# Transposed value weights of a backward kernel: DMA transposes from DRAM in place of TensorE transposes

## The chip, the cores and the metric

The kernel runs on one NeuronCore of a Trainium2 chip. The metric is device time in microseconds (us) of one execution; three executions before the change took 2987.54, 2988.93 and 2990.67 us, so the median is 2988.93 us. A core has a matrix engine (PE, TensorE), whose weight loads are shown apart (PEld), a vector engine (DVE), a scalar engine (ACT), a general one (POOL) and a sync engine (SP) that issues DMAs. SP, ACT and POOL each have their own DMA queue; sixteen DMA engines move the data of all queues.

## The reference, cut to what matters

The kernel computes the forward pass and all weight and input gradients of a transformer block. Half A is a recurrent-memory attention (32 heads of 128, model width 512, 2048 rows in segments of 32 with 8 memory rows); half B is a gated linear unit (GLU) of width 1792.

```python
def _A_ref(x, mem0, Wq, Wk, Wv, Wo, seg_len):      # Wq, Wk, Wv: [512, 32, 128]
    for s in range(n_seg):
        h = jnp.concatenate([mem, xs], axis=1)
        q = jnp.einsum('btd,dhe->bhte', h, Wq)
        k = jnp.einsum('btd,dhe->bhte', h, Wk)
        v = jnp.einsum('btd,dhe->bhte', h, Wv)
        ...
        o = jnp.einsum('bhte,hed->btd', o, Wo)
        mem = o[:, :M, :].copy()
def _B_ref(x, w_gate, w_up, w_down):
    h = _sigmoid(jnp.einsum('bsd,df->bsf', x, w_gate)) * jnp.einsum('bsd,df->bsf', x, w_up)
    return jnp.einsum('bsf,fd->bsd', h, w_down)
...
_out, _vjp = jax.vjp(_f, A_x, A_mem0, A_Wq, A_Wk, A_Wv, A_Wo, B_w_gate, B_w_up, B_w_down, c, w_mod)
_grads = _vjp(grad_out)
```

The gradient of `h` in half A needs products with the transposed weights, such as `dv` times `Wv` with `d` as the result's axis. For these the kernel keeps `WqT`, `WkT` and `WvT` in SBUF, each 128 partitions (the head's axis `e`) by 32 heads by 512, and `WoT` likewise. They are made from the weights in DRAM; what is at issue here is how `WvT` is made.

## The kernel before, in words

The work comes in stages one after the other: forward attention (phase 2), the GLU forward and its input gradients (phase 3), the GLU weight gradients with the making of the transposed weights (the stage of this case, lines 1426 to 1489), the attention backward over the 64 segments in reverse (phase 4), and the attention's weight gradients (phase 5).

**The stage.** The gradient of `w_down` is finished first (line 1369). Then, from 1342.6 to 1471.6 us of the profiled span, come the gradients of `w_gate` (from `DGROWS`) and `w_up` (from `DUROWS`). Each is cut into four column chunks of 448. The text calls them DG0 to DG3 and DU0 to DU3. A chunk is four groups `c` of 16 matmuls (line 1470): `h2r` as weights, a chunk `xr` of the rows as the moving operand, into a PSUM tile `gps` of which there are four. Each group's result is copied out by ACT or DVE in turn (`ot`, two tiles) and stored by a DMA on POOL's queue. A chunk of rows is 1792 KB in DRAM; there are two such tiles in SBUF (`ring`), and `load_xr` (line 1448) issues the load of chunk i+2 on ACT's queue when the matmuls of chunk i have all read. After DU0 and DU1, 16 matmuls of the first attention backward step are put in (`first_dO_pass`), and after DU2 eight transposes (`first_dO_turns`).

**The weight pieces.** Between the groups, PE makes the transposed weights in 32 pieces of four heads, handed out evenly over the stage by `emit_setup`: eight of `Wq`, eight of `Wo`, eight of `Wk`, eight of `Wv`. A piece of `Wq`, `Wk` or `Wv` is one DMA on SP's queue of 512 KB from DRAM into one of four slots (line 1559), 16 transposes on PE (line 1564, four to a PSUM tile `wtp`, of which there are two), and four copies of 128 by 512 from PSUM to `WqT`, `WkT` or `WvT`, two of three on DVE and the third on ACT. A slot's next load waits until the transposes of the piece four places before have read it, so SP runs about four pieces ahead of PE.

**What sets the order.** SP's order in this stage is pinned to the order of the code. A scheduler orders the other engines and gives each DMA of SP and ACT one of eight completion semaphores (in the built program `DMAHW0` to `DMAHW7`), shared by the two queues. A DMA waits before it is issued until the DMA that had its semaphore before has landed. An engine works strictly in its own order, so whatever stands behind a waiting DMA on ACT or SP waits too.

**After the stage.** Phase 4 first loads `Pst`, `OT`, `Qst` and `Kst` on SP's queue and `VT` on ACT's; `WvT` is first read by PE at 1478.98 us of the profiled span (line 215).

The text calls the pieces of `Wk` K0 to K7 and those of `Wv` V0 to V7.

Of the kernel before, what the change touches and what calls it, by code (L numbers as in the profile page):

```python
# [40 lines left out]
class K:  # L41
# [1496 lines left out]
    def p4_weights_setup_pieces(self, ctx):  # L1538
        nc, tc, cfg, io = self.nc, self.tc, self.cfg, self.io
        D, DC, H, E = cfg.D, cfg.DC, cfg.H, cfg.E  # L1540
        HB = 4
        sps = ctx.enter_context(tc.tile_pool(name="p4sps", bufs=2, space=PSUM, reuse_waits="tile"))
        pieces = []
        kk = [0]
        n, NT = DC * HB * E, cfg.NT
        slots = [self.flat(self.Wv, 2 * NT * 448, n)] + [self.flat(self.Wk, i * n, n) for i in range(3)]
        first = [slots[0], self.flat(self.Wk, NT * D, n), slots[0], slots[0]]
        np_ = [0]

        def slot(pat, **kw):  # L1550
            np_[0] += 1
            t = first[np_[0] - 1] if np_[0] <= 4 else slots[(np_[0] - 4) % 4]
            return t.rearrange(pat, **kw)

        def qkv_piece(src_ap, dst, h0):
            def f():
                srcv = src_ap.rearrange("(c p) h e -> p c h e", p=128)
                wn = slot("p (c h e) -> p c h e", c=DC, e=E)
                nc.sync.dma_start(wn, srcv[:, :, h0:h0 + HB, :])
                for hi in range(HB):  # L1560
                    h = h0 + hi
                    tp = sps.tile([128, DC, 128], BF16, name="wtp")
                    for c in range(DC):
                        nc.tensor.transpose(tp[:, c, :], wn[:, c, hi, :], self.ident[:])
                    self.evac("dve" if kk[0] % 3 != 2 else "act", dst[:, h, :], tp[:, :, :].rearrange("p c d -> p (c d)"))
                    kk[0] += 1
            return f

        def wo_piece(h0):
            def f():  # L1570
                wov = io["A_Wo"].rearrange("h e d -> e h d")
                won = slot("p (h d) -> p h d", h=HB)
                nc.sync.dma_start(won, wov[:, h0:h0 + HB, :])
                for c in range(DC):
                    tp = sps.tile([128, HB, 128], BF16, name="wtp")
                    for i in range(HB):
                        nc.tensor.transpose(tp[:, i, :], won[:, i, c * 128:(c + 1) * 128], self.ident[:])
                    self.evac("dve" if kk[0] % 3 != 2 else "act", self.WoT[:, c, h0 * E:(h0 + HB) * E],
                              tp[:, :, :].rearrange("p i e -> p (i e)"))
                    kk[0] += 1  # L1580
            return f

        for (src_ap, dst) in ((io["A_Wq"], self.WqT), (None, None), (io["A_Wk"], self.WkT), (io["A_Wv"], self.WvT)):
            for h0 in range(0, H, HB):
                pieces.append(wo_piece(h0) if dst is None else qkv_piece(src_ap, dst, h0))
        return pieces

    def p4_weights_setup_transposes(self):
# [817 lines left out]
```

## Time and profile before

| what | value |
|---|---|
| median of three runs | 2988.93 us |
| the profiled execution | 2995.39 us, span 2993.6 us |
| PE busy over the span | 2930.3 us (98%) |
| transposes of line 1564 | 384 (128 of them for `Wv`), 1303.4 to 1469.0 us |
| matmuls of line 1470 | 512, 1342.6 to 1471.3 us |
| loads of the DUROWS chunks, issued on ACT's queue | 1389.69, 1404.74, 1420.99, 1438.84 us |
| loads of `Wv` pieces, issued on SP's queue | 1418.5 to 1452.6 us |
| mean granted TensorE clock | 0.995 of full speed |

The profile has one row of records for each engine. Times are from the start of the span. A matmul's listed duration overlaps with the next one's, so the cost of a group is read from one start to the next, not from the durations' sum. "Granted clock" is the share of full speed at which TensorE was clocked in that stretch. The DMA share is the mean busy share of the sixteen DMA engines, and can exceed 1 where packets overlap.

### The profile page before, as it was taken

How to read it: one execution, taken by the hardware profiler on the slowest of the kernel's cores; microseconds unless marked ns; L12 is line 12 of the kernel's file. 1: busy time of each engine (PE TensorE's matmuls, PEld its weight loads, DVE VectorE, ACT ScalarE, POOL GpSimd, SP SyncE). 2: the span in 40 equal slices, each digit the busy share in tenths (PEclk: the TensorE clock that was granted, in tenths of full speed). 3: DMA queues.
4: the chain of work that ended last, by engine and by line, in shares of the span. 5: the costliest groups of instructions: out<-in, count | busy, mean ns of one | idle time of the engine just before them, and what ended most of it. 6: DMA issues, size and time to landing. Idle time of an engine off the chain costs nothing. (4 is left out here: it accounts for less than half of the span.)

```text
span 2993.6 us, 105831 instructions
## 1 busy us (share of the span) xinstructions
PE 2930.3 (98%) x43947; PEld 1838.7 (61%) x44021; DVE 1631.3 (54%) x3679; ACT 1271.0 (42%) x3057; POOL 1233.4 (41%) x2489
## 2 busy tenths in 40 slices
PE   6999999999999999999999999999999999999999
PEld 3666666666665544445677777677777754445544
DVE  5656666665655788833456565566556632750011
ACT  2555555555555533312355555455555520110011
POOL 2455555545555222221244444444444422762111
PEclk8999999999999999999999999999999999999999
DMA  9988988889989899998699999999999997786565
GB/s 306 213 226 216 211 214 224 210 218 214 210 215 271 214 233 229 230 282 281 201 247 251 250 252 250 243 252 251 252 253 253 248 280 247 250 263 190 162 213 168
DMA packets 836436, 703.04 MB, mean 235 GB/s; under 512 B 536642, under 2 KB 708850, under 8 KB 835060
## 3 DMA queue, kind: packets, MB, share of 16 engines
q1 hardware_dynamic: 710756, 486.09, 66.3%
q0 software_dynamic: 54640, 148.90, 15.9%
q10 hardware_dynamic: 70560, 61.28, 6.4%
q8 instruction: 346, 5.67, 0.8%
q14 instruction: 134, 1.10, 0.1%
HBM read 294.99 MB, written 276.35 MB: 191 GB/s over the span
## 5 line engine op out<-in xcount | busy, mean ns | idle before, releaser
L2187 PE MATMUL gps<-rows,hrows 128*128 128x512 bf16 (+2 forms) x2124 | 413.6, 355 | 1.9
L2187 PEld LDWEIGHTS <-hrows 128*128 128x128 bf16 x2160 | 211.2, 98 | 204.4 <-issue 0.9
L63 DVE CAST ot<-gps 128x512 bf16<-128x512 f32 (+3 forms) x76 | 48.2, 634 | 304.3 <-PE gps L2187 221.0
L1855 POOL COPY dOst<-RAd 96x512 bf16<-96x512 bf16 x128 | 75.2, 611 | 299.4 <-DVE RAd L63 297.3
L1038 POOL TENSOR_TENSOR Pst<-Pst,rden 120x1408 bf16<-120x1408 bf16 x63 | 159.7, 2535 | 83.9 <-issue 53.6
L61 ACT ACTIVATE ot<-gps 128x512 bf16<-128x512 f32 (+3 forms) x75 | 41.2, 549 | 349.9 <-PE gps L2187 220.1
L2191 POOL DMA_DIRECT2D out_dram<-ot x108 | 81.4, 754 | 260.2 <-DVE ot L63 137.0
L659 PE MATMUL pass_ps<-Wv,hT 128*32 128x512 bf16 (+2 forms) x2304 | 186.6, 357 | 0.0
L257 PEld LDWEIGHTS <-hT 128*32 128x32 bf16 x4096 | 115.2, 97 | 103.2 <-issue 6.0
L63 DVE CAST Vst<-pass_ps 96x512 bf16<-96x512 f32 x128 | 87.4, 683 | 106.7 <-ACT RBv L61 92.9
L215 PE MATMUL dh_ps<-WvT,dVT 128*32 128x512 bf16 x2048 | 133.9, 381 | 1.7
L223 PE MATMUL at_ps<-Wo,OT 128*32 128x256 bf16 x4096 | 124.6, 274 | 4.0 <-DMA Wo<-in_A_Wo_dram 3.4
L257 PE MATMUL pass_ps<-Wq,hT 128*32 128x512 bf16 x2048 | 124.0, 383 | 4.1 <-DMA Wq<-in_A_Wq_dram 4.1
L659 PE MATMUL pass_ps<-Wv,hb 128*32 128x512 bf16 (+2 forms) x636 | 127.2, 345 | 0.0
L257 PE MATMUL pass_ps<-Wk,hT 128*32 128x512 bf16 x2048 | 123.5, 383 | 2.5 <-POOL hT L549 1.1
L257 PE MATMUL pass_ps<-WoT,dyT 128*32 128x256 bf16 (+1 forms) x3072 | 122.7, 308 | 2.8 <-issue 2.0
L223 PE MATMUL dhq_ps<-WqT,dQT 128*32 128x256 bf16 x4096 | 122.9, 273 | 0.0
L215 PE MATMUL dh_ps<-WkT,dKT 128*32 128x512 bf16 x2048 | 122.3, 380 | 0.0
L2202 PE MATMUL gps5o<-WoT,rows 128*128 128x512 bf16 x549 | 120.4, 379 | 1.7 <-DMA rows<-OSR 1.1
L794 POOL DMA_DIRECT2D Vst<-RBv x192 | 99.6, 523 | 53.9 <-ACT ET L841 34.5
L223 PEld LDWEIGHTS <-dQT 128*32 128x32 bf16 x4096 | 110.0, 97 | 15.5
L315 DVE TENSOR_TENSOR dST<-dh_ps,dST 128x512 bf16<-128x512 f32 x64 | 44.3, 691 | 130.3 <-ACT dST L314 130.3
(472 smaller groups left out, 7037.8 us busy)
## 6 DMA issues: line engine op xcount, KB each, us to landing
OSR<-Ost SPq DMA_DIRECT2D x64, 352.0 KB
OT<-OT SPq DMA_DIRECT2D x64, 352.0 KB
PS<-Pst SPq DMA_DIRECT2D x64, 352.0 KB
Pst_l<-PS SPq DMA_DIRECT2D x64, 352.0 KB
OT_l<-OT SPq DMA_DIRECT2D x64, 352.0 KB
DVR<-rows_x POOLq DMA_DIRECT2D x64, 352.0 KB, 6.5
DKR<-rows_x POOLq DMA_DIRECT2D x64, 352.0 KB, 5.9
DQR<-rows_x POOLq DMA_DIRECT2D x64, 352.0 KB, 3.3
```

Of the source, the lines that this page charges most:

```text
L63: return nc.vector.tensor_copy(out, in_)
L215: self.nc.tensor.matmul(ps[32 * j:32 * j + 32, :], lhsT=lhsT, rhs=w, start=(n < 4), stop=(n >= total - 4), tile_position=(0, 32 * j))
L223: nc.tensor.matmul(ps[32 * j:32 * j + 32, :], lhsT=x[k], rhs=w[k][:, 256 * d:256 * d + 256], start=(n == 0), stop=(n == total - 1), tile_p ...
L257: self.nc.tensor.matmul(ps[32 * j:32 * j + 32, :], lhsT=lhs(c), rhs=rhs, start=(c == 0), stop=(c == DC - 1), tile_position=(0, 32 * j))
L315: nc.vector.tensor_tensor(lo, ps[:], hi, op=ALU.subtract)
L659: nc.tensor.matmul(ps[32 * j:32 * j + 32, o * E:(o + n) * E], lhsT=lhsT, rhs=wc[:, 3 * a + hl:3 * (a + n - 1) + hl + 1:3, :], start=(c == ...
L794: nc.gpsimd.dma_start(Vst[96 + 8 * j:104 + 8 * j, :], rb[32 * j + o:32 * j + o + 8, :])
L1038: nc.gpsimd.tensor_tensor(Pst[0:120, :, :], Pst[0:120, :, :], rden[:, :].unsqueeze(2).to_broadcast([120, G, 128]), op=ALU.mult)
L1855: nc.gpsimd.tensor_copy(dOst[0:96, 512 * hf:512 * hf + 512], RAd[0:96, 512 * hf:512 * hf + 512])
L2187: nc.tensor.matmul(ps[:, 0:ng * E], lhsT=hrows[:, tp_, c * 128:(c + 1) * 128], rhs=rows[:, tp_, 0:ng * E], start=(tp_ == 0), stop=(tp_ == ...
L2191: nc.gpsimd.dma_start(outw[c * 128:(c + 1) * 128, h0:h0 + 3 * (ng - 1) + 1:3, :], ot[:, 0:ng * E].rearrange("p (h e) -> p h e", e=E))
L2202: nc.tensor.matmul(pss[gg][:], lhsT=rows[:, t, gg * E:(gg + 1) * E], rhs=dyrows[:, t, :], start=(n == 0), stop=(n == NTP - 1))
```

## The change

The pieces of `Wv` are no longer loaded plainly and transposed by PE. Each is instead four DMA transposes on SP's queue, straight from DRAM into `WvT`: 128 rows by 512 columns (128 KB) that land as four blocks of 128 by 128. That is 32 DMA transposes for 8 plain loads, 128 PE transposes and 32 copies out of PSUM. The order of the pieces changes too: `Wq`, `Wo`, K0 to K3, and then four times one piece of `Wk` followed by two of `Wv`. The number of pieces and how `emit_setup` hands them out stay as they are, but the last twelve places now hold only four pieces with work for PE.

```diff
+        def dma_piece(src_ap, dst, h0):
+            def f():
+                for c in range(DC):
+                    nc.sync.dma_start(dst[:, h0:h0 + HB, c * 128:(c + 1) * 128],
+                                      src_ap[c * 128:(c + 1) * 128, h0:h0 + HB, :].rearrange("p h e -> p (h e)"), transpose=True)
+            return f
+
+        heads = range(0, H, HB)
+        pieces = [qkv_piece(io["A_Wq"], self.WqT, h0) for h0 in heads] + [wo_piece(h0) for h0 in heads]
+        ks = [qkv_piece(io["A_Wk"], self.WkT, h0) for h0 in heads]
+        vs = [dma_piece(io["A_Wv"], self.WvT, h0) for h0 in heads]
+        pieces += ks[:4]
+        for i in range(4):
+            pieces += [ks[4 + i], vs[2 * i], vs[2 * i + 1]]
-        for (src_ap, dst) in ((io["A_Wq"], self.WqT), (None, None), (io["A_Wk"], self.WkT), (io["A_Wv"], self.WvT)):
-            for h0 in range(0, H, HB):
-                pieces.append(wo_piece(h0) if dst is None else qkv_piece(src_ap, dst, h0))
         return pieces
```

In the built program the rest of the instructions keep their order on every engine. The semaphores of the stage's DMAs are handed out anew. The load of DU1's rows now has the semaphore that V0's first transpose had before it (`DMAHW4`), the load of DU2's rows that of V5's third transpose (`DMAHW5`), and the load of DU3's rows that of V6's second (`DMAHW1`). Before the change, the loads of DU1 to DU3 shared theirs with the loads of O6, K2 and K6 (O6 the seventh piece of `Wo`), all issued more than 8 us earlier.

## The prediction

> **What bounds the kernel now.** I read the page's busy rows first, then the line of the transposes, the order in time on PE, SP and ACT between 1380 and 1480 us, and last the stretches' DMA share and clock.
>
> ```profile
> PE 2930.3 (98%) x43947; PEld 1838.7 (61%) x44021; DVE 1631.3 (54%) x3679; ACT 1271.0 (42%) x3057; POOL 1233.4 (41%) x2489
> L1564 PE MATMUL wtp<-ident,Wv x128: 216/219/219, 1303.7 to 1469.0; 128*128 128x128 bf16 x128
> ```
>
> PE is busy nearly always, so a transpose taken out of its stream counts, if nothing else ends the stage later. The order in time on PE (start, duration, what) gives the price:
>
> ```profile
> 1432.19 2.62 PE L1470 MATMUL gps<-Wv,Wk 128*128 128x448 bf16 x13
> 1434.64 0.61 PE L1564 MATMUL wtp<-ident,Wk 128*128 128x128 bf16 x8
> ...
> 1436.18 2.62 PE L1470 MATMUL gps<-Wv,Wk 128*128 128x448 bf16 x13
> 1438.73 1.05 PE L257 MATMUL pass_ps<-WoT,dyb 128*32 128x512 bf16 x16
> 1439.71 3.20 PE L1470 MATMUL gps<-Wv,Wk 128*128 128x448 bf16 x16
> ```
>
> Thirteen matmuls take 2.45 us from start to start (1432.19 to 1434.64), so one takes 0.189 us and a group of 16 takes 3.03. V0's stretch, 1434.64 to 1438.73, holds 16 matmuls and 16 transposes: 4.09 us, so the piece costs 1.06.
>
> The moving rows come on ACT's queue, and nothing waits for them now: of 512 matmuls one waited 0.4 us. DU2's load is the third line:
>
> ```profile
>   DMA Wv<-DGROWS: 0.4, 1
> 1404.74 0.37 ACTq L1448 DMA_DIRECT2D Wv<-DUROWS  x1
> 1420.99 0.37 ACTq L1448 DMA_DIRECT2D Wv<-DUROWS  x1
> 1399.43 13.31 SPq L1559 DMA_DIRECT2D Wk<-in_A_Wk_dram  x3
> L1197 SPq DMA_TRANSPOSE hdT<-h x14: 1201/1202/1227, 994.6 to 1242.5; - x14
> 1424.00:1426.00 2.00, 2.00 (x12) 1.07 (x11) 0.00 (x0) 0.31 (x1) 0.00 (x0) 1.00 1.10 386
> ```
>
> ACT's queue moves data for DU2's load from 1422.2 to 1429.7 us (the DMA queues by single microseconds), so it lands about 8.7 us after its issue and 10.0 us before DU2's first matmul at 1439.71. SP issues K4's load at 1399.43. The nearest row to the new DMAs is `hdT<-h`: the same 128 by 512 into four blocks, but out of SBUF; it holds SP for 1.20 us. A full-rate plain load moves 386 GB/s (last number).
>
> **The change part by part.** The profiled execution took 2995.39 us (span 2993.6), 6.5 us or 0.22% above the median of 2988.93. All terms are differences, so I add them to the median. About 0.2% (6 us) is what a measurement of this kernel can tell from no change.
>
> *Taken off PE.* Eight pieces. From one piece's first transpose to the next's, less 3.03 us for 16 matmuls (and 0.45 for the eight turns after DU2), V0 to V7 cost 1.06, 1.07, 0.95, 0.96, 1.01, 1.21, 0.89, 1.08: together 8.2. Small waits between stretches of matmuls add a few tenths; I take **-8.6**, as laying out the stage anew gives it (below). The 32 copies out of PSUM (0.42 us on DVE, 0.60 on ACT) and eight plain loads (0.37 us each on SP) go too. Those engines were waiting for PE here, so they save nothing.
>
> *Added on SP.* 32 DMA transposes of 128 KB. Plain loads of DRAM and stores to DRAM hold their issuer equally long (0.37 and 0.36 us), so I carry the 1.20 us over from an SBUF source to a DRAM source; two in a row start 1.29 us apart (1242.55, 1243.84). 32 make 41 us of SP. They do not run in the last quarter: SP is not held back until a place comes up, but only by the slots of K4 to K7, and those are free when K0 to K3 are turned, which K4's issue at 1399.43 shows for K0. So V0 is issued at 1399.9 and the rest follow at SP's pace. Data: in a stretch with little else, transposes move 190 to 233 GB/s, so 4.19 MB need 20 us of all DMA engines where plain loads needed 11. Spread over 41 us this is half of them. While DU1's load also runs (7 us at full share), 128 KB at half of 190 GB/s take 1.38 us, 0.09 more than an issue, which delays the stream by some **0.5**.
>
> *The wait that it adds.* This decides. In the built program DU2's load, on ACT's queue, has taken over the completion semaphore of V5's third transpose and waits until that has landed. That is the 23rd transpose. With K5's and K6's loads between (0.46 each), its issue ends at 1399.9 + 23 x 1.29 + 0.9 + 0.5 = 1431.0. Data of an `hdT` transpose run 0.7 us from the end of issue; `rows_x<-dQT` among other loads was landed 4.4 us after it (issue to 2431.79, its reader at 2436.22). I take 2.5, so 1433.5, where ACT could issue at 1420.99 before. Behind the wait on ACT stand the copies of DU1's first and third group, of the first pass and of one head of K5, and DU3's load. POOL's stores wait for these copies and DVE's copy of the fourth group for a store. But there are four `gps` tiles and two `wtp`, so PE gets through DU1 and stops only where it needs DU2's rows. These take 8.7 us as now, or with nine transposes beside them some 9: landed at 1442.5.
>
> *PE anew.* DU0 ends at 1420.8 as now (V0 would stand behind it). The first pass takes 1.0, DU1 64 x 0.189 + 1.0 for K5 = 13.1, the second pass 1.0: PE wants DU2's rows at 1435.9 where it wanted them at 1439.7. From there DU2, turns and DU3 with K6 and K7 take 26.8, so without a wait the stage ends at 1462.7 to 1463 instead of 1471.57 (the -8.6). With rows at 1442.5 PE stands still for **+6.6**.
>
> *The clock after it.* When PE stood 1.6 us after several smaller gaps, its clock was 0.50 from 1477 to 1480:
>
> ```profile
> 1476.07 0.37 PE L1810 MATMUL g_ps<-Pst_l,dOst 128*128 128x120 bf16 x4 [1.57 <-DMA Pst_l<-PS]
> 1477.00:1477.50 0.50, 0.50 (x8) 0.50 (x6) 0.19 (x1) 0.04 (x1) 0.00 (x0) 0.50 0.83 274
> 1480.50:1481.00 0.50, 0.50 (x13) 0.07 (x6) 0.00 (x0) 0.00 (x0) 0.00 (x0) 1.00 0.97 355
> ```
>
> 3.6 us at half clock are **+1.8** after a stand of 6.6 us. That dip itself, at phase 4's start, stays: its cause is the load of `Pst`, which waits for PE's last `gps` matmul as before.
>
> *The rest.* DU1's load waits for V0's first transpose, landed by 1403.6, before its own time of 1404.74: nothing. DU3's load waits for V6's second, landed near 1438, and then follows DU2's on the queue, landed near 1449 for a need at 1456: nothing, with 7 us of cover. K5 to K7 are issued at 1410, 1421 and 1432, each over 10 us before its turn. `WvT` is complete near 1446, read at 1479.
>
> Sum: -8.6 + 6.6 + 1.8 = **-0.2 us**, so 2988.7.
>
> *The unknown price.* The trace has no DMA transpose out of DRAM. Each 0.1 us on the interval moves the end by 2.3. From below, the issue of a copy (0.37) would leave the data rate (128 KB at 190 GB/s, 0.69) as the bound: V5's third would land at 1419, no wait. From above, the slowest transpose that shows is `duT<-du` at 1277.85, 448 KB in 6.08 us, or 1.74 for 128 KB, 1.83 with the gap: +12.4; landing at 4.4 instead of 2.5 adds 1.9. I take 1.29 as the row of the same shape, and keep both ends.
>
> The Trainium skill (DMA: Bandwidth & Descriptors, the table within "Why a DMA increments its semaphore by 16 and not by 1") gives the issue of a small DMA transpose from HBM to SBUF as 631 cycles before trn3; at the 1.2 GHz that its page Trainium Kernel Development and Optimization (NeuronCore Architecture) gives for SyncEngine, I estimate 0.53 us from the two pages. No run here shows it. By it the sum would be -8.6.
>
> **The rivals.**
>
> *Transposes out of DRAM are issued quickly.* Mechanism: the 23rd transpose lands before DU2's load needs to go. With the interval at or below 1.0 us it lands at 1427, and rows are there at 1436: the gain is whole, 2988.9 - 8.6 = **2980.3**. It decides below 1.08, where wait and dip leave less than -6. For it: a copy is issued in 0.37, so the 1.20 is work on transposing, which may be cheaper from DRAM. Against: `hdT<-h` never took under 1.20.
>
> *Transposes out of DRAM are slower, so the wait of DU2's load outgrows the gain.* Place: ACT's queue ahead of DU2; price 2.3 us for each 0.1; it decides from 1.56 us on (+6). At 1.83 and a late landing: 2988.7 + 12.4 + 1.9 = **3003**. For it: 256-byte packets (3146 of 3170 packets under 512 bytes while transposes ran) read out of rows 8 KB apart; the medians of 1.80 and 2.02 us for `rows_x` of 352 KB among other traffic. Against: those are 2.75 times as much data.
>
> *The wait binds nothing.* If DU2's load went at 1421 as now, the result would be that of the first rival; only the semaphore's count speaks against it, and I fold it in there.
>
> **How the numbers follow.** Wait about as long as the gain: 0.42, **2988.7**, its own range 2983 to 2995. Quick issue: 0.22. Slow: 0.36. The range leaves 0.1 below for nothing but scatter of the first rival, hence 2979, and 0.1 above, beyond the slow rival's 3003, hence 3008. Faster by over 0.2%: 0.23; within: 0.41; slower: 0.36.
>
> **What would show it.** No line for `Wv` among the transposes, PE's stage after 1399 shorter by 8.6 us of work; SP's transposes 1.2 to 1.3 us each from 1399.9 on; DU2's load issued near 1433 and not 1421, at the landing of the 23rd; one wait of PE of some 7 us at line 1470 for the rows of `DUROWS`; a granted clock of 0.5 for 3 to 4 us behind it. I am wrong if DU2's load is issued before 1427 (faster), if the transposes take over 1.5 us each (slower), or if a second wait shows at DU3 or at `WvT`'s first reading.

## The result, and the profile after

The changed kernel takes 2996.35 us (median of 11 runs, 2992.21 to 3001.48), the kernel before 2989.11 on the same chip. The ratio is 1.0020, with an interval of 1.0011 to 1.0028: it is slower by 3 to 8 us. The forecast was 2988.7, no change; the time lies in the range, on the side of the rival with slow transposes. The profiled execution of the changed kernel took 2996.40 us (span 2994.6). That of before was itself 0.22% above its median, so the two profiles are compared by stage, not by span.

The ruler for the stage is the same in every profile below: from the moment SP stands at the load of Wq's third piece (before the change has any effect) to PE's first matmul of phase 4. In the kernel before these are 1305.67 and 1471.58 us, 165.91 apart; after, 1306.46 and 1477.66, 171.20 apart. So the stage became **5.3 us longer**, which is the whole change within the interval.

The page of the changed kernel, busy time by engine, and the source line of the new transposes (shortest, median and longest time for which one holds SP, in ns):

```profile
PE 2922.9 (98%) x43819; PEld 1831.5 (61%) x43893; DVE 1623.0 (54%) x3657; ACT 1264.4 (42%) x3047; POOL 1232.4 (41%) x2489
L1586 SPq DMA_TRANSPOSE WvT<-in_A_Wv_dram x32: 1200/1267/4027, 1400.5 to 1449.6; - x32
```

PE has 128 instructions and 7.4 us of work fewer, as the change says. A transpose out of DRAM holds SP for 1.27 us at the median; 1.20 was carried over from the SBUF source, and that was right. What was not foreseen is the longest, 4.03. The order in time on SP (start, duration) shows where it lies:

```profile
1400.49 11.04 SPq L1586 DMA_TRANSPOSE WvT<-in_A_Wv_dram  x8
1411.63 0.86 SPq L1559 DMA_DIRECT2D Wk<-in_A_Wk_dram  x1
1412.54 13.75 SPq L1586 DMA_TRANSPOSE WvT<-in_A_Wv_dram  x8
1426.39 0.53 SPq L1559 DMA_DIRECT2D Wk<-in_A_Wk_dram  x1
1426.96 10.36 SPq L1586 DMA_TRANSPOSE WvT<-in_A_Wv_dram  x8
```

Eight undisturbed transposes take 10.36 us (the third group, which K6's load of 512 KB did not hold). The second group takes 13.75, and the first of it alone 4.03, while DU1's rows, issued at 1405.45, are being loaded. The 23rd transpose, seventh of the third group, so ends its issue at 1426.96 + 7 x 1.295 = 1436.0. The order in time on ACT then has DU2's rows load, and the copy behind it with the wait that both went through:

```profile
1405.45 0.37 ACTq L1448 DMA_DIRECT2D Wv<-DUROWS  x1
...
1437.69 0.37 ACTq L1448 DMA_DIRECT2D Wv<-DUROWS  x1
1438.10 0.60 ACT L61 ACTIVATE RBd<-pass_ps 128x512 bf16<-128x512 f32 x1 [17.90 <-DMA WvT<-in_A_Wv_dram]
```

ACT stood 17.9 us for a transpose on another queue, and the rows load that went at 1420.99 before now goes at 1437.69. The order in time on PE shows what that costs:

```profile
1436.05 1.05 PE L257 MATMUL pass_ps<-WoT,dyb 128*32 128x512 bf16 x16
1449.05 7.97 PE L1470 MATMUL gps<-Wv,Wk 128*128 128x448 bf16 x32 [11.96 <-DMA Wv<-DUROWS]
1456.86 0.61 PE L1564 MATMUL wtp<-ident,Wk 128*128 128x128 bf16 x8
```

PE stands 12.0 us at DU2's first matmul, from 1437.1 on, and the next 32 matmuls take 7.81 us from start to start, where 32 x 0.189 = 6.05 are due. The stretches of 2 us (busy time of PE, PEld, DVE, ACT and POOL, then granted clock, DMA share and GB/s) tell why:

```profile
1440.00:1442.00 2.00, 0.00 (x0) 0.00 (x0) 0.00 (x0) 0.00 (x0) 0.50 (x1) 1.00 1.07 322
1442.00:1444.00 2.00, 0.00 (x0) 0.00 (x0) 0.00 (x0) 0.00 (x0) 0.00 (x0) 0.59 1.11 339
1448.00:1450.00 2.00, 0.95 (x3) 0.43 (x4) 0.08 (x1) 0.00 (x0) 1.86 (x4) 0.50 1.27 274
1452.00:1454.00 2.00, 2.00 (x10) 0.98 (x9) 0.00 (x0) 0.00 (x0) 0.00 (x0) 0.85 1.16 325
```

The clock falls to 0.50 near 1442.4, 5.3 us into the stand, and returns near 1452.6, 3.6 us after PE resumed: +1.8 us. With the eight pieces gone from PE, -8.6 + 12.0 + 1.8 = +5.2, against 5.3 by the ruler.

### The profile page after: what moved, and what is told of

Its sections match the earlier page's. It is cut to its first block, busy times and chain, and to the rows that moved or that the text cites. A ratio compares the mean times of both kernels' runs of the same rounds, so it can differ in the third digit from the quotient of the medians.

```text
span 2994.6 us, 105557 instructions
## 1 busy us (share of the span) xinstructions
PE 2922.9 (98%) x43819; PEld 1831.5 (61%) x43893; DVE 1623.0 (54%) x3657; ACT 1264.4 (42%) x3047; POOL 1232.4 (41%) x2489
## 4 chain that ended last, share of the span: by engine, by line
PE 77%; issue 10%; DMA 5%; DVE 3%; POOL 3%; SPq 1%; ACT 1%; POOLq 0%; DVEq 0%; ACTq 0%
PE pass_ps L257 14%; PE dh_ps L215 8%; PE g_ps L1821 5%; PE pass_ps L659 5%; PE gps5o L2213 4%; PE dhq_ps L223 4%; PE at_ps L223 4%; PE mm L1291 3%; PE dh_tps L215 3%; PE gps L1470 2%; POOL out_dram L2202 2%; PE turn_ps L829 2%; PE mm L1251 2%; PE mm L1266 2%; PE tps L1738 2%
## 5 line engine op out<-in xcount | busy, mean ns | idle before, releaser
L1470 PE MATMUL gps<-Wv,Wk 128*128 128x448 bf16 x512 | 108.1, 357 | 12.2 <-DMA Wv<-DUROWS 12.0
```

Source lines behind the costliest of these rows:

```text
L1470: nc.tensor.matmul(ps[:], lhsT=h2r[:, j, c * 128:(c + 1) * 128], rhs=xr[:, j, :], start=(j == 0), stop=(j == NT - 1))
```

## The experiments

Theory S: the loss is the wait for the shared semaphore, and without it the 8 to 9 us of the transposes are gained. Theory C: the transposes burden the DMA engines, so that other transfers land late, whichever queue or semaphore they have. All ratios are to the kernel before, on the same chip; "stage" is the ruler's change against 165.91 us, read from the one profiled execution of each kernel, so a few tenths there say little.

| kernel | rows of DU2, DU3 on | value weights | tiles for copies | ratio, interval | stage, us |
|---|---|---|---|---|---|
| changed kernel | ACT | 32 x 128 KB | 2 | 1.0020, 1.0011 to 1.0028 | +5.3 |
| rows on POOL | POOL | 32 x 128 KB | 2 | 0.9999, 0.9990 to 1.0008 | +0.7 |
| three tiles alone | ACT | 32 x 128 KB | 3 | 1.0020, 1.0011 to 1.0029 | +5.3 |
| POOL and three tiles | POOL | 32 x 128 KB | 3 | 0.9969, 0.9957 to 0.9981 | -9.6 |
| before, three tiles | ACT | on PE | 3 | 0.9993, 0.9984 to 1.0002 | -1.0 |
| plain copies | ACT | 32 x 128 KB, not transposed | 2 | 0.9970, 0.9959 to 0.9981 | -9.0 |
| order alone | ACT | on PE, new order | 2 | 1.0004, 0.9995 to 1.0013 | 0.0 |
| sixteen transposes | ACT | 16 x 256 KB | 2 | 0.9987, 0.9976 to 0.9999 | -0.4 |
| eight transposes | ACT | 8 x 512 KB | 2 | 0.9982, 0.9973 to 0.9991 | -5.9 |
| eight, three tiles | ACT | 8 x 512 KB | 3 | 0.9974, 0.9965 to 0.9983 | -9.8 |
| spread | ACT | 32 x 128 KB, spread | 2 | 0.9985, 0.9971 to 0.9998 | -5.1 |
| spread, sixteen | ACT | 16 x 256 KB, spread | 2 | 0.9975, 0.9964 to 0.9985 | -7.8 |
| spread, sixteen, three tiles | ACT | 16 x 256 KB, spread | 3 | 0.9962, 0.9949 to 0.9974 | -8.6 |
| spread, eight, three tiles | ACT | 8 x 512 KB, spread | 3 | 0.9990, 0.9981 to 0.9998 | +2.2 |

A last kernel, with a quarter of DU1's load, stands at the end; it leaves out three quarters of DU1's rows and ran once, so only its transposes are read.

### DU2's and DU3's rows on POOL's queue

```diff
-                    nc.scalar.dma_start(t, rows[:, ch * CH:(ch + 1) * CH].rearrange("(j p) f -> p j f", p=128))
+                    (nc.gpsimd if i >= 6 else nc.scalar).dma_start(t, rows[:, ch * CH:(ch + 1) * CH].rearrange("(j p) f -> p j f", p=128))
```

> The loads of DU2's and DU3's rows go out on POOL's queue, which has other completion semaphores; the DMA transposes stay as they are. Theory S (DU2's load stood on a semaphore shared with V5's third transpose, from 1421 to 1437.7 us): the load is issued near 1422 to 1423, lands by 1435 even if it takes the 11.4 us that it took beside the transposes, PE's wait of 12.0 us and the half clock behind it go, and the stage keeps the 8.4 us of transposes: 2981 us, 0.27% under before. Theory C (the transposes' packets crowd the rows out of the DMA engines, whatever the issue): PE still waits 5 us or more at line 1470 and the time stays at 2990 to 2996 us.

DU2's load went at 1421.43, and the 12-us wait was gone. The time only returned to that of before. The waits in 1340 to 1480 us (us in total, times, longest) say what took the place:

```profile
DVE ot L63 <- DMA out_dram<-ot: 18.4, 5, 8.8
ACT ot L61 <- DMA out_dram<-ot: 12.4, 2, 8.7
PE wtp L1564 <- DVE WkT L63: 3.8, 2, 3.3
PE wtp L1564 <- ACT WkT L61: 2.9, 2, 2.3
PE gps L1470 <- DMA Wv<-DUROWS: 1.6, 1, 1.6
```

DVE and ACT wait 30.8 us in all for stores of `ot` tiles; a copy of a weight tile (`WkT`) stands behind such a wait on the same engine, its `wtp` bank stays taken, and PE waits for it. PE's waits of these three lines add up to 8.3 us, about the gain. In order of time on POOL, DVE and PE, with a stretch of 2 us:

```profile
1422.61 0.55 POOL L1475 DMA_DIRECT2D out_dram<-ot  x1
1432.43 0.62 DVE L63 CAST ot<-gps 128x448 bf16<-128x448 f32 x1 [3.48 <-DMA out_dram<-ot]
1433.44 0.38 PE L1564 MATMUL wtp<-ident,Wk 128*128 128x128 bf16 x4 [3.29 <-DVE WkT L63]
1436.00:1438.00 2.00, 2.00 (x7) 0.82 (x6) 0.00 (x0) 0.54 (x1) 0.54 (x1) 0.50 0.61 136
```

Behind PE's wait of 3.3 us the clock was 0.50 for 3.4 us (1434.8 to 1438.2), another 1.7 us. So -8.6 + 8.3 + 1.7 = +1.4, where the ruler gives +0.7. The store of 1422.61 landed 9.7 us after its issue; it went out right behind DU2's rows, on the same queue. The waits of 8.8 and 8.7 us end at 1457.0 and 1457.4, for stores issued behind DU3's rows (1440.73), which PE could use from 1456.63 on. So this run did two things: it took the shared semaphore away and put 1792 KB ahead of the stores on POOL's queue. The kernel before with its rows there was not run, and how much of the stores' lateness here is the transposes' stays open.

In the kernel before, the copies waited 2.9 us for stores in the same stretch, and a store landed 3.0 us after its issue (median of 1400 to 1440); in the changed kernel this is 6.7, here 7.9. These medians are of the few stores whose landing the profile tells. So theory S was right on the wait and wrong on the gain. Theory C was right on the time, but had not named the stores, and its 5 us of PE at line 1470 were 1.6.

### Plain copies in the transposes' place, and the order alone

```diff
-                                      src_ap[c * 128:(c + 1) * 128, h0:h0 + HB, :].rearrange("p h e -> p (h e)"), transpose=True)
+                                      src_ap[c * 128:(c + 1) * 128, h0:h0 + HB, :])
```

> The same 32 DMAs from the same places of DRAM to the same places of SBUF, at the same points of SP's order, but as plain copies; WvT then holds untransposed blocks, so the transposing is left out and gradients that use it change. Theory S: an issue takes 0.37 us instead of 1.27, SP is through with the sixth piece before 1415, DU2's load goes at 1421 and nothing waits: 2981 us, 0.27% under before. Theory O (it is not the transposing but the 32 DMAs on SP and their semaphores as such): DU2's load is still issued after 1430 and the time stays above 2990 us.

The same bytes at the same places, the turning left out. SP by time:

```profile
1398.91 6.37 SPq L1586 DMA_DIRECT2D WvT<-in_A_Wv_dram  x8
1406.06 0.37 SPq L1559 DMA_DIRECT2D Wk<-in_A_Wk_dram  x1
1406.47 11.44 SPq L1586 DMA_DIRECT2D WvT<-in_A_Wv_dram  x8
```

Undisturbed, eight take 6.37 us in place of 10.36. Beside DU1's load they are held too (11.44). In this program DU2's load shares its semaphore with K6's load, issued at 1418.01, and not with the 23rd copy; it went at 1423.85, 2.9 us later than before. PE did not wait for rows, and the stage lost 9.0 us: the eight pieces are worth what the forecast said, if nothing else comes late. With both the semaphore and the transposing changed, the run does not tell S from C; the four corners below do in part.

```diff
-        vs = [dma_piece(io["A_Wv"], self.WvT, h0) for h0 in heads]
+        vs = [qkv_piece(io["A_Wv"], self.WvT, h0) for h0 in heads]
```

> The new order of the pieces alone: four times one piece of Wk and two of Wv at the end, all of them plain loads with transposes on PE. Theory S: as before, 2989 us within 2 us, DU2's load issued at 1421. Rival theory O2 (the order itself costs, by WkT being finished last or by the eviction engines' turns): 2 to 7 us slower.

Old way of loading, new order: no difference in time (1.0004) or stage (0.0). The order alone costs nothing.

### Fewer and larger transposes at the same places

```diff
-        def dma_piece(src_ap, dst, h0):
+        def dma_piece(src_ap, dst, h0, n=8):
+                if h0 % n:
+                    return
-                    nc.sync.dma_start(dst[:, h0:h0 + HB, c * 128:(c + 1) * 128],
-                                      src_ap[c * 128:(c + 1) * 128, h0:h0 + HB, :].rearrange("p h e -> p (h e)"), transpose=True)
+                    nc.sync.dma_start(dst[:, h0:h0 + n, c * 128:(c + 1) * 128],
+                                      src_ap[c * 128:(c + 1) * 128, h0:h0 + n, :].rearrange("p h e -> p (h e)"), transpose=True)
```

> Sixteen DMA transposes of eight heads (256 KB) instead of 32 of four heads (128 KB), at the places of every other piece: the same bytes and packets, half the instructions and semaphores. In the built program DU2's load then waits for the tenth of the sixteen. Theory S: at 1.4 to 2.2 us each that lands between 1418 and 1426 us, DU2's load goes 11 to 16 us sooner than in the changed kernel, its rows are there at 1430 to 1437, PE waits 0 to 2 us: 2981 to 2984 us. Theory C: the same bytes crowd the rows out as much, PE waits 8 us or more, 2992 to 2997 us.

DU2's load waits for the 10th of sixteen transposes and goes at 1428.99. In order of time on PE:

```profile
1441.88 7.91 PE L1470 MATMUL gps<-Wv,Wk 128*128 128x448 bf16 x32 [4.38 <-DMA Wv<-DUROWS]
```

A wait of 4.4 us in place of 12.0, with the same dip of the clock behind it (7.91 us for 32 matmuls); the stage is back at that of before (-0.4). This lies between the theories: S had expected 2 us at most, C 8 or more. The runs scatter from 2979.15 to 2992.98 us, so one profiled execution says less here than elsewhere. With n=16 the scheduler hands DU2's load the semaphore of the fourth of eight transposes:

> The value columns come in eight transposes of 512 KB in place of thirty-two of 128 KB, at the same places of the order; same bytes. The scheduler then hands DU2's rows load a semaphore whose last user is the fourth of these eight, not one near the end of the third group. Theory S (only the shared semaphore costs): the load is issued at about 1421, PE waits for it no longer, and the stage ends about 8 us earlier than in the kernel before: ratio 0.9972. Theory C (the transposes slow what else the DMA engines carry, rows and stores, whatever the semaphores): a wait of PE of 2 to 6 us in all stays in 1400 to 1450, for rows or for copies that wait for stores, and the ratio is 0.9990 to 1.0005. The long issue, 1.2 us for each 128 KB, should show as some 4.5 to 5.5 us for each 512 KB by both.

DU2's load went at 1425.51, PE did not wait for rows, and the stage lost 5.9 us, the time 0.18%. With DU2's rows still on ACT's queue, more than half of the gain comes with the wait gone, but not all: the copies still waited for stores,

```profile
DVE ot L63 <- DMA out_dram<-ot: 17.8, 4, 7.5
```

which is theory C's remainder. The next run takes that away with a third tile.

```diff
-            op_ = ctx.enter_context(tc.tile_pool(name="p3g_o", bufs=2, reuse_waits="tile"))
+            op_ = ctx.enter_context(tc.tile_pool(name="p3g_o", bufs=3, reuse_waits="tile"))
```

> The eight transposes of 512 KB, and three tiles in place of two for the gradient's copies out of PSUM (a store that lands late then holds a copy one tile later). Theory C with the stores as its path: the copies' waits for stores in 1400 to 1450 fall from over 10 us to under 4, PE waits under 1 us, ratio 0.9975. Theory C with the rows as its path: nothing changes against the eight transposes alone. Theory S: both kernels at 0.9972.

No copy waited for a store any more, and the stage lost 9.8 us. By time alone the two kernels' intervals overlap (0.9982 and 0.9974); the difference of 3.9 us is read from the stage, and 1.0 of it a third tile gives the kernel before as well (the control below). So with the rows on ACT's queue, late stores cost some 2.9 us.

### The four corners: rows on ACT or POOL, two tiles or three

> The kernel before with three tiles in place of two for the gradient's copies out of PSUM, and nothing else: a control for the runs with three. If the stores held the copies in the kernel before too, it gains up to 2 us (0.9993); if, as its stores' landings of 3 to 4 us and its waits in the stage say, they did not, it is the same, 0.9995 to 1.0005.

The control: in the kernel before a third tile changes nothing that the time can tell (0.9993, interval to 1.0002; stage -1.0).

> The changed kernel's thirty-two 128-KB transposes in their old places, DU2's and DU3's rows on POOL's queue (which took the 12-us wait away and gained nothing), and now three tiles for the copies. Theory C with the stores as its path (late stores hold the copies, the copies the PSUM banks, the banks PE): the copies' waits for stores fall from 28 us in all to under 8, PE's waits from about 8 us to under 3, and the gain of the transposes comes back, 5 to 9 us: 0.9970 to 0.9983. Theory C with the rows or the weights themselves late: 0.9995 to 1.0000, as with two tiles.

The changed kernel's own thirty-two transposes, and 9.6 us off the stage, 8.6 of them beyond the control, as much as the term of the eight pieces. The stores still land late, 8.0 us at the median of eight, but now only one wait is left of them:

```profile
ACT ot L61 <- DMA out_dram<-ot: 3.2, 1, 3.2
```

PE runs from DU1 through DU2 without an idle line:

```profile
1434.14 1.05 PE L257 MATMUL pass_ps<-WoT,dyb 128*32 128x512 bf16 x16
1435.12 6.23 PE L1470 MATMUL gps<-Wv,Wk 128*128 128x448 bf16 x32
```

> The changed kernel with three tiles in place of two for the copies, and nothing else: DU2's rows load stays on ACT's queue, behind the same semaphore of the 23rd transpose. If the shared semaphore is a loss of its own, PE's wait for DU2's rows stays at 10 to 12 us with the dip of the clock behind it, and the time is 1.001 to 1.0025, as with two tiles (1.002). If late stores were the whole loss, the wait of PE is gone or under 3 us and the ratio is 0.997 to 0.998, as with three tiles and the rows on POOL's queue (0.9969).

The fourth corner gained nothing: 1.0020 and a stage of +5.3, as with two tiles. Its waits:

```profile
ACT RBd L61 <- DMA WvT<-in_A_Wv_dram: 18.9, 1, 18.9
DVE ot L63 <- DMA out_dram<-ot: 14.6, 1, 14.6
PE gps L1470 <- DMA Wv<-DUROWS: 12.6, 1, 12.6
```

DVE's wait is part of the same stand: POOL's stores come in order, and the next one waited for a copy on ACT. So the two losses do not add up; the first hides the second. With the shared semaphore, PE stands for rows, and a third tile is worth nothing. Without it, and with the rows on POOL's queue ahead of the stores, the stores bind and cost nearly the whole gain. Only both away give it back.

### The order spread

```diff
-        pieces = [qkv_piece(io["A_Wq"], self.WqT, h0) for h0 in heads] + [wo_piece(h0) for h0 in heads]
-        ks = [qkv_piece(io["A_Wk"], self.WkT, h0) for h0 in heads]
+        pieces = [qkv_piece(io["A_Wq"], self.WqT, h0) for h0 in heads]
+        ks = [wo_piece(h0) for h0 in heads] + [qkv_piece(io["A_Wk"], self.WkT, h0) for h0 in heads]
...
-        pieces += ks[:4]
-        for i in range(4):
-            pieces += [ks[4 + i], vs[2 * i], vs[2 * i + 1]]
+        for i in range(8):
+            pieces += [ks[2 * i], ks[2 * i + 1], vs[i]]
```

> The order alone is another: after Wq's eight pieces two of Wo's or Wk's and then one value piece, eight times, so that the value pieces' groups of four 128-KB transposes lie some 14 us apart over 110 us and not four in each 6 us over 50 us. Theory C: a group of four (5 us of issue) meets one rows load or store at most and the queue never backs up, so the waits stay under 2 us in all and 6 to 8 us are gained: ratio 0.9975. Theory S: DU2's rows load now shares its semaphore with DU1's load, issued 16 us before, so it is not late, and DU3's with a transpose late in the stage: a wait of up to 5 us can come there; ratio 0.9972 to 0.9990.

DU2's load went at 1417.05, with no wait for rows; the stage lost 5.1 us. Copies waited for stores still (14.1 us in all), and PE for copies of `WkT` and `WqT` 3.6. That the queue would never back up was wrong: the longest of the transposes held SP 3.30 us.

> The spread order, with sixteen transposes of 256 KB, four in every other value place. Theory C: groups of 9 us of issue (four of 256 KB at about 1.8 to 2 us) collide with rows loads more than groups of 5 us do, so it should lie between the spread order with 128-KB transposes and the sixteen in the changed kernel's order (0.9987): 0.9978 to 0.9987. Theory S: no rows load but DU3's waits for a transpose of its own time; 0.9972.

7.7 us of waits for stores, stage -7.8. The guess that groups of larger transposes collide more was wrong by these two ratios (0.9975 against 0.9985), though their intervals overlap.

> Spread order, sixteen transposes of 256 KB (0.9975 with two tiles), and three tiles. Stores held copies there for 7.7 us in all, the longest 3.5, and PE waited little: so three tiles bring at most 1 to 2 us, 0.9969 to 0.9975.

The fastest of all, 2980.23 us, 0.9962, and faster than the 0.9969 to 0.9975 expected: no copy waited for a store, and PE waited 0.9 us for rows. By its interval (0.9949 to 0.9974) it beats both kernels; against the other kernels at 0.997 it is not told apart.

> Spread order, eight transposes of 512 KB, three tiles: all that has helped, together. If each removes its own part of the same loss there is nothing left to gain beyond what plain copies in the transposes' place gave (9 us of the stage): 0.9970 to 0.9975, as the eight transposes with three tiles in the changed kernel's order (0.9974). If spreading and tiles add up, 0.9965.

This one missed clearly. 512-KB transposes in the spread order fall beside the loads of Wo's pieces. On SP and, next, on PE in order of time:

```profile
1350.58 24.87 SPq L1588 DMA_TRANSPOSE WvT<-in_A_Wv_dram  x4
```

```profile
1383.70 1.03 PE L1577 MATMUL wtp<-ident,Wk 128*128 128x128 bf16 x8 [9.12 <-DMA Wk<-in_A_Wo_dram]
```

Four transposes held SP for 24.9 us, the Wo load behind them was issued at 1375.56, and PE waited 9.1 us for it. The same queue that here carries transposes carries the weights that PE turns next, so a group must be shorter than the head start of the load behind it.

### What held the transposes: DU1's load cut to a quarter

```diff
-                    nc.scalar.dma_start(t, rows[:, ch * CH:(ch + 1) * CH].rearrange("(j p) f -> p j f", p=128))
+                    nj = NT // 4 if i == 5 else NT
+                    nc.scalar.dma_start(t[:, :nj], rows[:nj * 128, ch * CH:(ch + 1) * CH].rearrange("(j p) f -> p j f", p=128))
```

> DU1's rows load (1.79 MB, issued 5 us after the first transpose) brings only its first quarter; the rest of DU1's product is left out of the computation in effect, since its rows are those of an older load. For the transposes' stream alone: if DU1's load is what holds it, the first transpose of the second group takes 1.3 to 1.6 us in place of 4.03, the group of eight 10.3 to 11 in place of 13.75, and the third group starts at about 1423.5 in place of 1427.0. If the transposes hold themselves (or K5's load does it), the second group stays at 13 to 14 us. DU2's rows load now shares its semaphore with the 25th transpose, not the 23rd, so PE's wait for it stays by both, at some 8 to 12 us, and the time of the whole says nothing.

SP by time:

```profile
1394.91 11.15 SPq L1587 DMA_TRANSPOSE WvT<-in_A_Wv_dram  x8
1406.16 0.52 SPq L1560 DMA_DIRECT2D Wk<-in_A_Wk_dram  x1
1406.73 10.37 SPq L1587 DMA_TRANSPOSE WvT<-in_A_Wv_dram  x8
1417.20 1.18 SPq L1560 DMA_DIRECT2D Wk<-in_A_Wk_dram  x1
1418.43 10.37 SPq L1587 DMA_TRANSPOSE WvT<-in_A_Wv_dram  x8
```

The second group takes 10.37 us in place of 13.75, and the third starts 23.52 us after the first in place of 26.47. (By the clock it starts at 1418.43 and not at the 1423.5 expected, since this whole stage ran 5.6 us earlier: the first transpose went at 1394.91, not 1400.49.) So DU1's rows load, on ACT's queue, holds the transposes on SP's queue for 2.95 us. (The shorter load also went earlier, at 1397.47, 2.6 us after the first transpose in place of 5.0.) The first group, which K4's load goes before, stays at 11 us, and K6's load is held longer, 1.18.

## Why the prediction was wrong, step by step

*Taken off PE, -8.6:* right. It comes back as 8.6 where both waits are away (9.6 less the control's 1.0), and as 9.0 with plain copies. The row `wtp<-ident,Wv` and the sign "no line for `Wv`" were misread: there `Wv` names the storage of a slot that pieces of all four weights pass through (from 1303.7 us on, long before V0), and after the change the row is still there, with 96 in place of 128. The count over all slots tells it, 384 before and 256 after.

*Added on SP, 1.29 us from start to start, V0 at 1399.9:* right on the single transpose: 1.267 median, 1.295 in an undisturbed group, and the first at 1400.49 where this execution ran 0.59 us later (K4's load at 1400.02 against 1399.43). The Trainium skill (DMA: Bandwidth & Descriptors, "Why a DMA increments its semaphore by 16 and not by 1") would have made it 0.53 us by the prediction's estimate from its 631 cycles; the runs do not agree, no transpose was below 1.19 us, and the measurement decides. Of the two rivals' conditions, "quick issue" is refuted. "Slow transposes" has its direction but not its reason: one alone is not slow, the stream beside DU1's load is: 23 of them with two loads between took 35.5 us, and 33.8 without these two loads (0.86 and 0.53 on SP and the 0.3 of gaps), 1.47 each.

*Which delays the stream by some 0.5, while DU1's load runs:* **the step that failed.** I had let the load and a transpose share the data rate, and found 0.09 us each. The stream was 4.9 us late at the third group's start (26.47 us after V0 where 16 x 1.29 + 2 x 0.46 = 21.56 were due), 4.4 more than allowed; 2.95 of it are shown to be DU1's load. The rest lies in the first group (11.04 against 10.3) and in the slower issue of the plain loads; what held these was not tried.

*The shared semaphore:* right, and shown from both sides. DU2's load went at 1437.69, 1.7 us after the 23rd transpose's issue, where I had 2.5 for the landing. Put on POOL's queue it went at 1421.43.

*Rows in some 9 us, beside nine transposes:* **too low.** From issue to PE's start it was 11.4 us. So the stand of 6.6 us became 6.6 + 4.4 (the stream) - 0.8 (the landing) + 2.4 (the rows) - 0.6 (PE came there later) = 12.0. The stream's and the rows' sizes make the difference between "same" and "slower". That DU1's load slows the transposes is shown; that transposes slowed these rows is argued, since K7's load and the stores held back till then came beside them too.

*The clock, +1.8:* right, 1.76. The Trainium skill (TensorE: Matmul & The Clock Gate, "Part 1: The HAM clock gate") says that full clock comes back after some 3.4 us of sustained work; the 3.6 us here agree. That the dip at phase 4's start stays was wrong: in the changed kernel the clock is 1.00 from 1476 to 1490, where before it was 0.50 for 3.4 us. Phase 4's first products with `WkT` (line 215) start 11.20 us after the ruler's end in place of 12.01, 0.8 us that the ruler does not see.

*The rest at nothing:* right for K5 to K7, DU1's and DU3's loads and `WvT`, none of which PE waited for. I had DVE's copy waiting for a store, and counted on four `gps` tiles to cover it; that held here only because PE stood for longer. The stores' landing, 3.0 us before and 6.7 after (medians of a few stores each), I did not price.

*The rival with quick issue, 2980.3:* its result would not have come, had the load of DU2 gone in time with these transposes. Rows on POOL point to it: with the wait gone the time was as before (0.9999), because of the stores, though there the rows went ahead of them on POOL's queue. Eight transposes with the rows left on ACT lost less to the stores, 2.9 us. "If nothing waits, the gain is whole" left out that the stores can come late too. The 2980.3 itself, a ratio of 0.9971, is about what the runs with neither wait give: 0.9969 and 0.9962.

## What to carry to other kernels

When DMAs are added to a stage, ask for each transfer beside them (loads, and the stores that free a tile) how much later it may land, and read its slack from the trace; an issue time measured alone says little about a stream beside 1.8-MB loads. Look in the built program for DMAs on different queues that share a completion semaphore: it ties a load to a stranger's landing, and moving the load to another queue, or changing the number of DMAs, undoes it; but a load moved to another queue goes ahead of what stands there. When a removed wait brings nothing, take the next one in line away too before the theory is given up: here two waits hid each other. Rows on POOL alone gained nothing, a third tile alone nothing, both together 9.6 us.

## What the runs showed that was not expected

- Larger transposes cost less issue for their bytes. Undisturbed, 128 KB took 1.295 us of SP (10.36 for eight), 256 KB 1.69 (6.76 for four, the third group of the sixteen): 101 and 155 GB/s. The Trainium skill (DMA: Bandwidth & Descriptors, "Latency and other measured facts") gives 261 GB/s for transposes with a non-contiguous middle dimension; no undisturbed group out of DRAM came near that here.
- Beside a store the DMA engines were busier for fewer bytes. In the changed kernel:

```profile
1424.00:1426.00 2.00, 2.00 (x13) 1.00 (x11) 0.00 (x0) 0.00 (x0) 0.00 (x0) 1.00 1.22 126
1434.00:1436.00 2.00, 2.00 (x12) 0.88 (x9) 0.00 (x0) 0.00 (x0) 0.00 (x0) 1.00 0.44 98
```

  The second line is transposes alone: 0.20 MB at a share of 0.44. In the first they move 0.14 MB at a share of 0.75, beside 0.11 MB on POOL's queue at 0.47, a store issued at 1422.98. Beside loads the engines moved more: 354 GB/s at 1.33 from 1414 to 1416, while DU1's rows came. Which resource they contend for is not visible here and stays open.
- How much later a store lands because of the transposes is not shown by the landings. Their median in 1400 to 1440 is 6.7 us in the changed kernel, 7.9 and 8.0 with rows on POOL and 3.0 before; but with the order alone, which has no DMA transpose in this stage, it is 5.4 (four stores). The copies' waits for stores in 1340 to 1480 say more: 2.9 us before, 3.2 with the order alone, 8.4 with plain copies, 17.8 with eight transposes, 30.8 with rows on POOL.
